# Changing the PSUM banks and the column split of one batch's hidden layer in a fused attention and MLP kernel

## The chip, the cores and the metric

The kernel runs on one core of a Trainium2 chip. The metric is device time in microseconds of one execution. The kernel before the change was timed in three runs: 244.94, 244.96 and 245.18 us, median 244.96 us. One more execution was recorded by the hardware profiler; its rows are what the text below calls the trace.

## What is computed

Eight batches of eight heads, 576 tokens and head size 64. A short sequence `p` of 32 positions per head attends to the tokens, and the tokens then attend to the 32 packed results. The output, 512 wide, goes through a two-layer network with the activation h * cos(h). Cut to its core:

```python
def sm_attn(qq, kk, vv):
    s = scale * qq @ kk.T
    a = exp(s - max(s)); a = a / sum(a)
    return a @ vv
pp  = sm_attn(p, k, v)          # 8 x 8 x 32 x 64
o   = sm_attn(q, pp, pp)        # 8 x 8 x 576 x 64
x   = o.transpose(0, 2, 1, 3).reshape(4608, 512)
h   = x @ w_in                  # 4608 x 2048
out = (h * cos(h)) @ w_out      # 4608 x 512
```

## The kernel before, in words

**Staging.** The kernel never forms `x`. For each batch b it folds the packed values into the first weight, `PPW[b] = pp @ w_in` (`ppw`, four blocks of 512 columns, n = 0 to 3), and keeps the normalised weights of the second attention, `a2n[b]` (128 rows x 2 x 576 tokens). The hidden layer of a batch is then `PPW.T @ a2n`, made in 16 pieces of 128 features, fc = 0 to 15. Each piece is two accumulated products (y = 0, 1). ScalarE (ACT) takes cos as Sin(x + pi/2) from PSUM into a `cosT` tile (three buffers), and VectorE (DVE) multiplies it with the piece in PSUM into `gT[b]`. The output layer is 16 matmuls of 512 columns per chunk of 128 tokens, four chunks per batch; the last 64 tokens of two neighbouring batches share a fifth chunk, whose input is `joint`.

**Order.** The order of the instructions on every engine is the order in which the program writes them. A batch has a "slot" (`slot`), the loop over its 16 pieces. Between the pieces, and in the stages before a slot, `fill(n)` puts n matmuls of an earlier batch's output layer, taken from the generators `out_first` (batch 0) and `out_gen` (the others). `slot` spreads the matmuls that are left by a list of weights, runs named hooks after given pieces, and at piece 10 adds the next batch's generator. So the number of output matmuls in `fill` calls ahead of slot 1 and in slot 1 add up to a constant: 33 ahead and 39 inside before the change.

**Hidden pieces.** There are two forms. `h_mm` (line 260) makes a piece over all 576 tokens, as two halves of 288 in the two banks of a pair: four matmuls of 288 columns (line 269), one cos over 576 (273) and one product over 576 (276); after pieces 7 and 15 GpSimd copies the last 64 tokens into `joint` (280). `h_one` (289) makes the first 512 tokens in a single bank: two matmuls of 512 columns (295), one cos (300), one product (301). Batch 0 uses `h_one`, and its last 64 tokens are made later, in slot 1, by `h_rest` (304): 32 matmuls of 64 columns into a pair (309), one cos and one product over 1024 columns (313, 315). Batches 1 to 7 use `h_mm`.

**PSUM.** Two of the eight banks are the output accumulators (`ot`, pool psO). The other six are handed out by `banks(kind)` (55): "pairs" gives three pairs (tags A0, A1, B), "single" six single banks (H0 to H5), "held" two pairs and two banks (psX) in which `out_first` holds chunks 2 and 3 of batch 0. Tags are used in a ring; a tile that takes a bank waits until the last reader of the tile before it is done. By the code, psX lies over H0 and H1, A0 over H2 and H3, A1 over H4 and H5, B over H0 and H1.

**Around the change** (lines 484 to 562). After batch 0's pieces: `fill(4)`, blocks 0 and 1 of `PPW[1]`, `fill(4)`, the load of the exp table, block 2, all three blocks evacuated half by ACT and half by DVE (lines 88 and 90, the helper `copy`). Then "held": 24 transposes of q of batch 1 (122), their copies to `qT`, the scores of the second attention (`s2`, 149), their sums (245), `fill`s, `normalise` (253, 255), the Sin table, and slot 1. Slot 1's hooks make block 3 of `PPW[1]`, batch 0's rest, the transposes of p (137) and of k of batch 2 (122), and issue two DMA transposes on SP's queue. When the 48th output matmul of batch 0 is in, chunk 3 is done and the pool goes from "held" to "pairs". After slot 1 come `fill(4)` and the first-attention scores of batch 2 (`s1(2)`, 149).

Of the kernel before, what the change touches and what calls it, by code (L numbers as in the profile page):

```python
# [15 lines left out]
def kernel(  # L16
# [32 lines left out]
    small = ctx.enter_context(tc.tile_pool(name="small", bufs=3))  # L49
    O = ctx.enter_context(tc.tile_pool(name="psO", bufs=2, space=PSUM))  # L50
    ctx.enter_context(tc.manual_schedule())
    psum = {"stack": ctx.enter_context(ExitStack())}

    pairs, turn = [], [0]

    def banks(kind):


        psum["stack"].close()
        for name, n in {"held": [("psX", 2), ("psA", 1)], "single": [("psH", 1)]}.get(kind, [("psB", 1), ("psA", 1)]):  # L60
            psum[name] = psum["stack"].enter_context(
                tc.tile_pool(name=name, bufs=n, space=PSUM, reuse_waits="tile"))
        pairs[:], turn[0] = (["A0", "A1"] if kind == "held" else ["A0", "A1", "B"]), 0

    banks("pairs")
    V, ACT, G = nc.vector, nc.scalar, nc.gpsimd
# [25 lines left out]
    def psa(dt=FP32):  # L92
        at = pairs[turn[0] % len(pairs)]
        turn[0] += 1
        return psum["ps" + at[0]].tile([128, 2, 512 if dt == FP32 else 1024], dt, name="psA", tag=at)
# [12 lines left out]

    def one(dt=FP32):
        turn[0] += 1  # L110
        return psum["psH"].tile([128, 512 if dt == FP32 else 1024], dt, name="psH", tag=f"H{(turn[0] - 1) % 6}")

    def pe_T(n, b, engs=(V, V, V), groups=(0, 1, 2), own=None):
        if 0 in groups:
# [186 lines left out]
            return lambda: V.tensor_tensor(out=gT[b][:, fc, 0:512], in0=ps, in1=cs, op=ALU.mult)  # L301
        return cos

    def h_rest(b):

        t = psa()
        for fc in range(NFC):
            for y in range(2):
                nc.tensor.matmul(t[:, fc // 8, (fc % 8) * 64:(fc % 8) * 64 + 64],
                                 PPW[b][:, y, fc * 128:(fc + 1) * 128], a2n[b][:, y, 512:576],  # L310
                                 start=(y == 0), stop=(y == 1))
        cs = cos_pool.tile([128, 2, 512], BF16, name="cosR", bufs=1)
        ACT.activation(out=cs, in_=t, func=AF.Sin, bias=PI_HALF)
        j0 = (b % 2) * 64
        V.tensor_tensor(out=joint[b // 2][:, :, j0:j0 + 64],
                        in0=t.rearrange("p a (f x) -> p (a f) x", x=64),
                        in1=cs.rearrange("p a (f x) -> p (a f) x", x=64), op=ALU.mult)

    osb_eng = [V]

# [44 lines left out]
    def out_first():  # L365

        pss = {}
        for c, fcs in ((0, 4), (1, 4), (2, 4), (3, 4), (0, 8), (1, 8), (2, 8), (3, 8),
                       (2, 12), (3, 12), (2, 16), (3, 16), (0, 16), (1, 16)):
            if c not in pss:  # L370
                pss[c] = (O if c < 2 else psum["psX"]).tile([128, DM], FP32, name="ot", tag="ot")
            for fc in range(8 if (c, fcs) in ((0, 16), (1, 16)) else fcs - 4, fcs):
                nc.tensor.matmul(pss[c], gT[0][:, fc, c * 128:(c + 1) * 128], w_out_bf[:, fc, :],  # L373
                                 start=(fc == 0), stop=(fc == NFC - 1))
                if fc == NFC - 1:
                    store(0, c, pss[c], V if c == 2 else ACT)
                    if c == 3:
                        banks("pairs")
                yield

    filler = []
# [101 lines left out]
    c15()()  # L483
    set_filler(0)
    fill(4)
    for n in range(2):
        ppw(1, n, (ACT, V), own=one)
    fill(4)
    ACT.preload_act_table_set(EXP_SET)
    ppw(1, 2, (ACT, V), own=one)  # L490
    banks("held")
    t = psa(BF16)
    for i in range(2):
# [10 lines left out]
    sums2(1, 0)  # L504
    fill(2)
    sums2(1, 1)
    fill(11)
    normalise(1)
    ACT.preload_act_table_set(SIN_SET)
    fill(4)  # L510
# [1 line left out]
    def slot(s, hooks, keep=0, heavy={}, last=None, trail=0, weight=None):  # L512

        left, done = to_do() - keep + trail, 0
        weight = weight or [1 + heavy.get(fc, (0, 0))[0] for fc in range(NFC)]
        for fc in range(NFC):
            rest = h_mm(s, fc)
            if fc == NFC - 1 and last:  # L520
                last()
            rest()
            if fc == 10 and trail:
                set_filler(s)
            quota = (left * sum(weight[:fc + 1])) // sum(weight) - done
            done += quota
            behind = min(quota, heavy[fc][1]) if fc in heavy else quota
            fill(quota - behind)
            while hooks and hooks[0][0] == fc:
                hooks.pop(0)[1]()  # L530
            fill(behind)
# [10 lines left out]

    def tk2():

        t = psa(BF16)
        later = []
        for i in range(2):
            later.append(pe_T("k", 2, (None,) * 3, (i,), own=lambda dt: t[:, i, :]))
        for eng, (out, ps) in zip((ACT, V), later):
            copy(eng, out, ps)  # L550

    def cross(n, b):
        return lambda: xbar(n, b)

    osb_eng[0] = ACT
    slot(1, [(5, lambda: ppw(1, 3, ACT)), (6, cross("k", 3)), (7, lambda: h_rest(0)), (9, cross("q", 2)),
             (10, lambda: pack_p(2, 4)), (12, tk2), (13, lambda: pe_T("k", 2, (V, V, ACT), (2,)))],
         trail=8, heavy={5: (0, 1), 7: (0, 4)}, weight=[3, 3, 3, 3, 3, 3, 2, 4, 2, 2, 1, 2, 1, 1, 3, 3])
    ACT.preload_act_table_set(EXP_SET)
    osb_eng[0] = V  # L560
    behind(xT["q", 2][0:1, 0, 0:1])
# [110 lines left out]
```

## Time and profile before

| | us |
|---|---|
| median of three runs | 244.96 |
| profiled execution | 244.77 |
| its span, first to last instruction | 243.0 |
| TensorE (PE) busy in the span | 233.1 |
| DVE busy | 161.9 |
| ACT busy | 167.0 |
| GpSimd (POOL) busy | 37.4 |
| slot 1 and the four output matmuls after it, by the trace | 43.38 to 64.12 |

The span lacks 1.77 us of the execution's time, which lie before the first and after the last instruction. PE is busy for 96% of the span; the granted PE clock is full in every slice. In rows of a timeline the first figure is the start and the second the length, both in us from the span's start. PEld is PE's weight load, which runs beside the matmuls. Matmuls overlap in PE's pipeline: one of 512 columns is listed with about 380 ns, but the next can start before it ends. So the cost of a matmul in a stream is the distance from one start to the next, and the rows of the chain of waits, which are cut that way, give it.

### The profile page before, as it was taken

The page shows a single profiled execution, that of the slowest core. Times are in us where ns is not written, and L with a number is a line of the kernel's source. Part 1 is how long each engine was busy: PE and PEld are TensorE (multiplying, and loading weights), DVE is VectorE, ACT ScalarE, POOL GpSimd, SP SyncE. Part 2 cuts the span into 40 slices and gives each one's busy share as a digit, 9 for nine tenths or more (in the row PEclk, how much of TensorE's full clock was granted, in tenths as well). Part 3 has the DMA queues.
Part 4 walks back from the last instruction along what each step waited for, and adds up shares of the span by engine and source line. Part 5 has one row for each costly group of instructions (what it writes and reads, how often), then busy time and mean ns, then how long its engine had stood idle before and what let it go on. Part 6 is the DMA issues. An engine that isn't in the chain of part 4 may idle for free.

```text
span 243.0 us, 5473 instructions
## 1 busy us (share of the span) xinstructions
PE 233.1 (96%) x2244; PEld 128.2 (53%) x2244; DVE 161.9 (67%) x256; ACT 167.0 (69%) x266; POOL 37.4 (15%) x60
## 2 busy tenths in 40 slices
PE   7789889999999999999999999999999999999994
PEld 3454335566545564566546564556456554565453
DVE  3359993568568886687857786677758787887001
ACT  2349899588749868876878677877788683776110
POOL 8522212210130005005100501030100110010000
PEclk9999999999999999999999999999999999999999
DMA  6999999999899999998999896989284102311133
GB/s 94 202 205 206 205 206 227 193 215 189 189 162 163 240 197 139 219 213 159 234 205 199 163 212 117 193 161 214 60 175 112 46 0 46 86 43 46 46 84 86
DMA packets 64376, 37.37 MB, mean 154 GB/s; under 512 B 36864, under 2 KB 59776, under 8 KB 64352
## 3 DMA queue, kind: packets, MB, share of 16 engines
q0 software_dynamic: 23152, 18.75, 51.5%
q1 hardware_dynamic: 40960, 18.16, 35.7%
q8 instruction: 17, 0.28, 0.5%
q10 hardware_dynamic: 240, 0.13, 0.2%
q14 instruction: 7, 0.06, 0.1%
HBM read 37.22 MB, written 9.44 MB: 192 GB/s over the span
## 4 chain that ended last, share of the span: by engine, by line
PE 83%; DVE 8%; ACT 3%; DMA 3%; issue 1%; ACTq 0%; POOLq 0%
PE ot L360 45%; PE psA L269 21%; PE ot L373 4%; DVE gT L301 3%; DMA kbf<-in_k_dram 3%; PE psA L219 3%; PE psA L149 2%; PE psA L245 2%; DVE gT L276 2%; DVE PPW L90 2%; PE ot L343 1%; PE psA L192 1%; PE psA L122 1%; ACT cosT L273 1%; DVE a2n L255 1%
## 5 line engine op out<-in xcount | busy, mean ns | idle before, releaser
L360 PE MATMUL ot<-w_out_bf,gT 128*128 128x512 bf16 x448 | 114.9, 379 | 0.0
L276 DVE TENSOR_TENSOR gT<-psA,cosT 128x576 bf16<-128x576 f32 x112 | 83.5, 757 | 22.2 <-ACT cosT L273 21.1
L273 ACT ACTIVATE cosT<-psA 128x576 bf16<-128x576 f32 x112 | 72.9, 652 | 25.1 <-PE psA L269 23.6
L269 PE MATMUL psA<-a2n,PPW 128*128 128x288 bf16 x448 | 73.2, 286 | 0.2 <-DVE gT L276 0.2
L360 PEld LDWEIGHTS <-gT 128*128 128x128 bf16 x448 | 42.2, 98 | 37.8 <-issue 4.2
L269 PEld LDWEIGHTS <-PPW 128*128 128x128 bf16 x448 | 43.8, 98 | 29.9 <-issue 1.0
L90 DVE CAST PPW<-psA 128x1024 bf16<-128x1024 f32 x19 | 23.0, 1221 | 7.9 <-PE psA L219 7.9
L90 DVE COPY osb<-ot 128x512 f32<-128x512 f32 (+2 forms) x18 | 11.7, 648 | 16.0 <-PE ot L343 14.6
L280 POOL COPY joint<-gT 128x512 bf16<-128x512 bf16 x14 | 8.6, 615 | 87.4 <-DVE gT L276 87.4
L88 ACT COPY osb<-ot 128x512 f32<-128x512 f32 (+1 forms) x20 | 11.3, 567 | 14.5 <-PE ot L360 12.2
L255 DVE SCALAR_TENSOR_TENSOR a2n<-a2u,r,lns 128x576 bf16<-128x576 bf16 x16 | 12.4, 815 | 12.3 <-ACT lns L253 12.3
L373 PE MATMUL ot<-w_out_bf,gT 128*128 128x512 bf16 x64 | 17.0, 380 | 0.3 <-DMA w_out_bf<-in_moe_w_out_dram 0.3
L158 ACT ACTIVATE a<-psA 128x576 bf16<-128x576 f32 x16 | 10.3, 647 | 7.7 <-PE psA L149 7.7
L247 ACT ACTIVATE lns<-psA 128x576 f32<-128x576 f32 x16 | 10.4, 651 | 7.4 <-PE psA L245 6.8
L360 PE MATMUL ot<-w_out_bf,joint 128*128 128x512 bf16 x48 | 14.6, 379 | 0.0
L237 ACT ACTIVATE a2u<-psA,rs 128x576 bf16<-128x576 f32 x16 | 11.0, 737 | 1.4 <-PE psA L149 1.4
L103 POOL COPY gate<-kT 1x1 bf16<-1x1 bf16 x4 | 0.7, 178 | 66.2 <-DMA kT<-kbf 66.2
L301 DVE TENSOR_TENSOR gT<-psH,cosT 128x512 bf16<-128x512 f32 x16 | 9.9, 685 | 0.4 <-ACT cosT L300 0.4
L253 ACT ACTIVATE lns<-lns 128x576 f32<-128x576 f32 x16 | 10.0, 673 | 0.0
L412 PE MATMUL ot<-wz 128*128 128x512 f32 (+2 forms) x13 | 7.7, 683 | 1.9 <-DVE wz L425 1.7
L300 ACT ACTIVATE cosT<-psH 128x512 bf16<-128x512 f32 x16 | 8.9, 631 | 0.7 <-DVE gT L301 0.7
L295 PE MATMUL psH<-a2n,PPW 128*128 128x512 bf16 x32 | 8.2, 381 | 1.0 <-DVE PPW L90 1.0
(89 smaller groups left out, 186.4 us busy)
## 6 DMA issues: line engine op xcount, KB each, us to landing
kbf<-in_k_dram POOLq DMA_DIRECT2D x8, 576.0 KB, 13.1
vbf<-in_v_dram POOLq DMA_DIRECT2D x8, 576.0 KB, 7.5
qbf<-in_q_dram POOLq DMA_DIRECT2D x8, 576.0 KB, 10.4
out_dram<-osb SPq DMA_DIRECT2D x24, 192.0 KB, 2.5
out_dram<-osb SPq DMA_DIRECT2D x22, 128.0 KB, 2.7
w_in_bf<-in_moe_w_in_dram POOLq DMA_DIRECT2D x4, 512.0 KB, 17.0
w_out_bf<-in_moe_w_out_dram POOLq DMA_DIRECT2D x4, 512.0 KB, 21.3
out_dram<-osb SPq DMA_DIRECT2D x25, 64.0 KB, 2.3
```

Of the source, the lines that this page charges most:

```text
L88: ACT.copy(out=out, in_=in_)
L90: eng.tensor_copy(out=out, in_=in_)
L158: ACT.activation(out=a1[b % 2][:, y, :, 0:TP].rearrange("p (e m) x -> p e m x", e=2), in_=ps[y][:, :, 0:HS].rearrange("p e (m x) -> p e m ...
L237: ACT.activation(out=a2u[b][:, y].rearrange("p (e x) -> p e x", e=2), in_=ps[y][:, :, 0:HS], func=AF.Exp, scale=rs1[b][:, y:y + 1])
L247: ACT.activation(out=lns[b][:, y].rearrange("p (e x) -> p e x", e=2), in_=ps[:, :, 0:HS], func=AF.Ln)
L255: V.scalar_tensor_tensor(out=a2n[b][:, y], in0=a2u[b][:, y], scalar=r1[b][:, y:y + 1], in1=lns[b][:, y], op0=ALU.mult, op1=ALU.mult)
L269: nc.tensor.matmul(ps[:, e, 0:HS], PPW[b][:, y, fc * 128:(fc + 1) * 128], a2n[b][:, y, e * HS:(e + 1) * HS], start=(y == 0), stop=(y == 1))
L273: ACT.activation(out=csv, in_=ps[:, :, 0:HS], func=AF.Sin, bias=PI_HALF)
L276: V.tensor_tensor(out=gT[b][:, fc, :].rearrange("p (e x) -> p e x", e=2), in0=ps[:, :, 0:HS], in1=csv, op=ALU.mult)
L301: return lambda: V.tensor_tensor(out=gT[b][:, fc, 0:512], in0=ps, in1=cs, op=ALU.mult)
L360: nc.tensor.matmul(ps, w, w_out_bf[:, fc, :], start=(fc == 0), stop=(fc == NFC - 1))
L373: nc.tensor.matmul(pss[c], gT[0][:, fc, c * 128:(c + 1) * 128], w_out_bf[:, fc, :], start=(fc == 0), stop=(fc == NFC - 1))
```

## The change

Batch 1's pieces are made by `h_one` instead of `h_mm`, in single banks. `h_rest` becomes `h_half(b, a)`: 16 matmuls of 64 columns for eight pieces into one single bank, one cos and one product over 512 columns. Slot 1 calls it four times, for both halves of batch 0 and of batch 1; the two copies into `joint` on GpSimd go. Slot 1 begins in a new layout "four" (single banks over H2 to H5, while psX still holds the two chunks) and goes to six single banks when the 48th output matmul is in, with the ring set to go on at H3. The single banks are reserved in order when the layout starts. Block 3 of `PPW[1]` moves from piece 5 to piece 7, into two single banks, evacuated by ACT and DVE instead of ACT alone; the transposes of p and k take single banks, and the third copy of k goes from ACT to DVE. Ahead of the slot, blocks 0, 1 and 2 of `PPW[1]` take H2 and H3, H0 and H1, H4 and H5 (before: H0 and H1, H2 and H3, H4 and H5), and two output matmuls move from `fill(11)` into the slot: 31 ahead, 41 inside. After the slot the layout is "pairs", its ring at A0.

```diff
@@ -49,18 +49,24 @@
     small = ctx.enter_context(tc.tile_pool(name="small", bufs=3))
     O = ctx.enter_context(tc.tile_pool(name="psO", bufs=2, space=PSUM))
     ctx.enter_context(tc.manual_schedule())
-    psum = {"stack": ctx.enter_context(ExitStack())}
-
-    pairs, turn = [], [0]
+    psum, inner, outer = {}, ctx.enter_context(ExitStack()), ExitStack()
+
+    pairs, turn, ring = [], [0], [6]
 
     def banks(kind):
 
 
-        psum["stack"].close()
-        for name, n in {"held": [("psX", 2), ("psA", 1)], "single": [("psH", 1)]}.get(kind, [("psB", 1), ("psA", 1)]):
-            psum[name] = psum["stack"].enter_context(
-                tc.tile_pool(name=name, bufs=n, space=PSUM, reuse_waits="tile"))
+        inner.close()
+        if kind != "four":
+            outer.close()
+        for name, n, st in {"held": [("psX", 2, outer), ("psA", 1, inner)], "four": [("psH", 1, inner)],
+                            "single": [("psH", 1, inner)]}.get(kind, [("psB", 1, inner), ("psA", 1, inner)]):
+            psum[name] = st.enter_context(tc.tile_pool(name=name, bufs=n, space=PSUM, reuse_waits="tile"))
         pairs[:], turn[0] = (["A0", "A1"] if kind == "held" else ["A0", "A1", "B"]), 0
+        ring[0] = 4 if kind == "four" else 6
+        if kind in ("four", "single"):
+            for i in range(ring[0]):
+                psum["psH"].tile([128, 512], FP32, name="psH", tag=f"H{i}")
 
     banks("pairs")
     V, ACT, G = nc.vector, nc.scalar, nc.gpsimd
@@ -108,7 +114,7 @@
 
     def one(dt=FP32):
         turn[0] += 1
-        return psum["psH"].tile([128, 512 if dt == FP32 else 1024], dt, name="psH", tag=f"H{(turn[0] - 1) % 6}")
+        return psum["psH"].tile([128, 512 if dt == FP32 else 1024], dt, name="psH", tag=f"H{(turn[0] - 1) % ring[0]}")
 
     def pe_T(n, b, engs=(V, V, V), groups=(0, 1, 2), own=None):
         if 0 in groups:
@@ -301,20 +307,19 @@
             return lambda: V.tensor_tensor(out=gT[b][:, fc, 0:512], in0=ps, in1=cs, op=ALU.mult)
         return cos
 
-    def h_rest(b):
-
-        t = psa()
-        for fc in range(NFC):
+    def h_half(b, a):
+
+        t = one()
+        for f in range(8):
+            fc = 8 * a + f
             for y in range(2):
-                nc.tensor.matmul(t[:, fc // 8, (fc % 8) * 64:(fc % 8) * 64 + 64],
-                                 PPW[b][:, y, fc * 128:(fc + 1) * 128], a2n[b][:, y, 512:576],
-                                 start=(y == 0), stop=(y == 1))
-        cs = cos_pool.tile([128, 2, 512], BF16, name="cosR", bufs=1)
+                nc.tensor.matmul(t[:, f * 64:f * 64 + 64], PPW[b][:, y, fc * 128:(fc + 1) * 128],
+                                 a2n[b][:, y, 512:576], start=(y == 0), stop=(y == 1))
+        cs = cos_pool.tile([128, 512], BF16, name="cosT")
         ACT.activation(out=cs, in_=t, func=AF.Sin, bias=PI_HALF)
         j0 = (b % 2) * 64
-        V.tensor_tensor(out=joint[b // 2][:, :, j0:j0 + 64],
-                        in0=t.rearrange("p a (f x) -> p (a f) x", x=64),
-                        in1=cs.rearrange("p a (f x) -> p (a f) x", x=64), op=ALU.mult)
+        V.tensor_tensor(out=joint[b // 2][:, 8 * a:8 * a + 8, j0:j0 + 64], in0=t.rearrange("p (f x) -> p f x", x=64),
+                        in1=cs.rearrange("p (f x) -> p f x", x=64), op=ALU.mult)
 
     osb_eng = [V]
 
@@ -375,7 +380,8 @@
                 if fc == NFC - 1:
                     store(0, c, pss[c], V if c == 2 else ACT)
                     if c == 3:
-                        banks("pairs")
+                        banks("single")
+                        turn[0] = 3
                 yield
 
     filler = []
@@ -483,11 +489,12 @@
     c15()()
     set_filler(0)
     fill(4)
-    for n in range(2):
+    for n, at in ((0, 2), (1, 0), (2, 4)):
+        turn[0] = at
+        if n == 2:
+            fill(4)
+            ACT.preload_act_table_set(EXP_SET)
         ppw(1, n, (ACT, V), own=one)
-    fill(4)
-    ACT.preload_act_table_set(EXP_SET)
-    ppw(1, 2, (ACT, V), own=one)
     banks("held")
     t = psa(BF16)
     for i in range(2):
@@ -504,7 +511,7 @@
     sums2(1, 0)
     fill(2)
     sums2(1, 1)
-    fill(11)
+    fill(9)
     normalise(1)
     ACT.preload_act_table_set(SIN_SET)
     fill(4)
@@ -516,7 +523,7 @@
         left, done = to_do() - keep + trail, 0
         weight = weight or [1 + heavy.get(fc, (0, 0))[0] for fc in range(NFC)]
         for fc in range(NFC):
-            rest = h_mm(s, fc)
+            rest = h_one(s, fc)() if s == 1 else h_mm(s, fc)
             if fc == NFC - 1 and last:
                 last()
             rest()
@@ -542,10 +549,9 @@
 
     def tk2():
 
-        t = psa(BF16)
         later = []
         for i in range(2):
-            later.append(pe_T("k", 2, (None,) * 3, (i,), own=lambda dt: t[:, i, :]))
+            later.append(pe_T("k", 2, (None,) * 3, (i,), own=one))
         for eng, (out, ps) in zip((ACT, V), later):
             copy(eng, out, ps)
 
@@ -553,9 +559,14 @@
         return lambda: xbar(n, b)
 
     osb_eng[0] = ACT
-    slot(1, [(5, lambda: ppw(1, 3, ACT)), (6, cross("k", 3)), (7, lambda: h_rest(0)), (9, cross("q", 2)),
-             (10, lambda: pack_p(2, 4)), (12, tk2), (13, lambda: pe_T("k", 2, (V, V, ACT), (2,)))],
-         trail=8, heavy={5: (0, 1), 7: (0, 4)}, weight=[3, 3, 3, 3, 3, 3, 2, 4, 2, 2, 1, 2, 1, 1, 3, 3])
+    banks("four")
+    slot(1, [(5, lambda: h_half(0, 0)), (6, cross("k", 3)), (6, lambda: h_half(0, 1)),
+             (7, lambda: ppw(1, 3, (ACT, V), own=one)), (9, cross("q", 2)), (9, lambda: h_half(1, 0)),
+             (10, lambda: pack_p(2, 4, one(BF16))), (11, lambda: h_half(1, 1)), (12, tk2),
+             (13, lambda: pe_T("k", 2, (None, None, V), (2,), own=one))],
+         trail=8, heavy={5: (0, 1), 6: (0, 1), 7: (0, 1), 9: (0, 1), 11: (0, 1)},
+         weight=[3, 3, 3, 4, 4, 2, 2, 2, 3, 2, 2, 2, 1, 2, 3, 3])
+    banks("pairs")
     ACT.preload_act_table_set(EXP_SET)
     osb_eng[0] = V
     behind(xT["q", 2][0:1, 0, 0:1])
```

## The prediction

> **What bounds the kernel now.** I read the page first, to see which engine fills the span.
>
> ```profile
> span 243.0 us, 5473 instructions
> ...
> PE 233.1 (96%) x2244; PEld 128.2 (53%) x2244; DVE 161.9 (67%) x256; ACT 167.0 (69%) x266; POOL 37.4 (15%) x60
> ...
> PE 83%; DVE 8%; ACT 3%; DMA 3%; issue 1%; ACTq 0%; POOLq 0%
> ```
>
> PE is busy nearly always, and the chain of waits that sets the end runs 83% through it. So time can be won by less PE work or where PE stands still, and nowhere else. Next the table of stretches, for slot 1 with the four output matmuls after it.
>
> ```profile
> 43.38:64.12 20.74, 20.23 (x176) 12.64 (x175) 14.58 (x20) 15.73 (x25) 2.21 (x3) 1.00 1.31 208
> ```
>
> Its columns are length, then busy time of PE, PEld, DVE, ACT and POOL. Busy PE hides short stops, because a matmul is listed longer than its share of the stream. What a matmul costs stands in the chain in order of time:
>
> ```profile
> 40.30 3.24 PE ot L373 x15
> ...
> 43.54 0.49 PE psA L269 x4
> ...
> 52.38 0.93 PE psA L309 x32
> ```
>
> A 512-column matmul takes 3.24/15 = 0.216 us of the stream, a piece in four matmuls of 288 takes 0.49, a 64-column one 0.93/32 = 0.029. With these I walked PE's timeline through slot 1 and looked for starts that come later than the one before plus its cost:
>
> ```profile
> 49.44 0.75 DVE L276 TENSOR_TENSOR gT<-psA,cosT 128x576 bf16<-128x576 f32 x1
> ...
> 49.56 0.59 PE L373 MATMUL ot<-w_out_bf,gT 128*128 128x512 bf16 x2
> ...
> 50.24 0.41 PE L219 MATMUL psA<-w_in_bf,ppT 64*32 64x512 bf16 x8
> ...
> 56.57 0.38 PE L373 MATMUL ot<-w_out_bf,gT 128*128 128x512 bf16 x1
> ...
> 57.12 0.65 PE L269 MATMUL psA<-a2n,PPW 128*128 128x288 bf16 x4 [0.17 <-DVE gT L276]
> ...
> 59.43 0.65 PE L269 MATMUL psA<-a2n,PPW 128*128 128x288 bf16 x4
> 59.52 0.76 DVE L276 TENSOR_TENSOR gT<-psA,cosT 128x576 bf16<-128x576 f32 x1 [0.27 <-ACT cosT L273]
> ...
> 60.33 0.50 PE L122 MATMUL psA<-ident,kbf 96*128 96x96 bf16 x8 [0.25 <-DVE gT L276]
> ...
> 62.52 1.67 PE L360 MATMUL ot<-w_out_bf,gT 128*128 128x512 bf16 x7
> ...
> 64.12 0.44 PE L149 MATMUL psA<-kT,P 64*32 64x288 bf16 x16
> ```
>
> There are three stops. Block 3 of PPW starts at 50.24 instead of 49.56 + 0.43 = 49.99: 0.25 late, just behind the product that ends at 50.19 and frees its pair. Of this 0.09 is the step from full to 64-row matmuls, which stays: at 64.12 it costs 64.12 - 62.52 - 7 x 0.216 = 0.09 with no bank in the way. That leaves **0.16**. Piece 11 starts at 57.12 instead of 56.79: **0.33**. The third group of k starts at 60.33 instead of 59.43 + 0.49 = 59.92: **0.41**, behind the product that ends at 60.28. All three wait for a pair of banks until the product in it is done. Together 0.90 us.
>
> **The change part by part.** *PE's work*: before, 16 x 0.49 + 0.93 = 8.77 us for batch 1's pieces and batch 0's rest. After, 32 x 0.216 + 64 x 0.029 = 8.77. The columns are the same, so nothing is won or lost here. The two output matmuls moved into the slot are neutral as well (33 + 39 = 31 + 41).
>
> *Ahead of the slot.* Here the pair that the q transposes take is freed one block sooner:
>
> ```profile
> 15.37 0.79 POOL L99 DMA_DIRECT2D qbf<-in_q_dram  x1 [3.45 <-PE psA L122]
> ```
> ```profile
> DMA to landing us min/median/max: 20.1/20.1/20.1
> ```
> ```profile
> 34.50 1.88 DVE L90 CAST PPW<-psH 128x512 bf16<-128x512 f32 x3
> ...
> 35.10 0.41 PE L219 MATMUL psH<-w_in_bf,ppT 64*32 64x512 bf16 x8
> ...
> 35.90 1.06 PEld L122 LDWEIGHTS <-qbf 96*128 96x128 bf16 x24 [0.69 <-DMA qbf<-in_q_dram]
> 35.93 0.84 PE L122 MATMUL psA<-ident,qbf 96*128 96x96 bf16 x16 [0.42 <-DVE PPW L90]
> 36.43 0.59 ACT L88 CAST PPW<-psH 128x512 bf16<-128x512 f32 x1
> 36.60 0.50 PE L122 MATMUL ot<-ident,qbf 96*128 96x96 bf16 x8
> ...
> 37.15 0.80 ACT L88 COPY qT<-ot 128x768 bf16<-128x768 bf16 x1
> ...
> 37.90 0.51 PE L149 MATMUL psA<-qT,ppT 64*32 64x288 bf16 x16
> ```
>
> DVE's three casts start 0.60 apart and end at 35.18, 35.78 and 36.38. The transposes wait for the second; after the change for the first, and then for q itself, whose load lands at 15.37 + 20.1 = 35.5. So they start at 35.5 instead of 35.93, 0.4 sooner. But the scores need the third copy of qT too, which is ACT's: it waits for the cast at 36.43, which sits behind a table load, and can start at 37.02, or at 36.92 if ACT's operations overlap as DVE's 0.68 at 0.60 apart do, instead of at 37.15. So the bounds are 0.13 by ACT and 0.40 by the transposes, and I take **0.2**, ACT's better case. The chain to `a2n` moves by as much:
>
> ```profile
> 41.60 1.55 DVE L255 SCALAR_TENSOR_TENSOR a2n<-a2u,r,lns 128x576 bf16<-128x576 bf16 x2 [3.83 <-ACT lns L253]
> ```
>
> With two output matmuls fewer, PE, which was there at 43.38, reaches the second matmul of piece 0 at 43.38 - 0.2 - 0.43 + 0.22 = 42.97, and `a2n` ends at 43.15 - 0.2 = 42.95. That costs some 0.03 us.
>
> *Evacuation.* The prices, by group and shape:
>
> ```profile
> L276 DVE TENSOR_TENSOR gT<-psA,cosT 128x576 bf16<-128x576 f32 x112 | 83.5, 757 | 22.2 <-ACT cosT L273 21.1
> L273 ACT ACTIVATE cosT<-psA 128x576 bf16<-128x576 f32 x112 | 72.9, 652 | 25.1 <-PE psA L269 23.6
> ...
> L301 DVE TENSOR_TENSOR gT<-psH,cosT 128x512 bf16<-128x512 f32 x16 | 9.9, 685 | 0.4 <-ACT cosT L300 0.4
> ...
> L300 ACT ACTIVATE cosT<-psH 128x512 bf16<-128x512 f32 x16 | 8.9, 631 | 0.7 <-DVE gT L301 0.7
> ...
> L315 DVE TENSOR_TENSOR joint<-psA,cosR 128x1024 bf16<-128x1024 f32 x1 | 1.2, 1225 | 0.6 <-ACT cosR L313 0.6
> L309 PEld LDWEIGHTS <-PPW 128*128 128x128 bf16 x32 | 1.1, 98 | 0.0
> ```
>
> DVE: before 16 x 0.757 + 1.225 = 13.3; after 20 x 0.685 = 13.7. The product of a half (512 columns into pieces of 64 of `joint`) isn't in the trace. It is bounded by half of L315, 0.61, and by the longer L276, 0.757; I take L301's 0.685, the same size. DVE also gets half of block 3 (0.68, a cast of those above) and the third copy of k (0.56, its row is with the rivals). In sum DVE gains 1.6 us, 14.6 to 16.2, in a stretch that PE fills for 19.8 (20.74 - 0.9). ACT: 20 x 0.631 = 12.6 against 16 x 0.652 and one of double width, at most 1.26, in sum 11.7; the copy of k (0.80, as that of qT above) and half of the block leave it. So it stays about where it is, 15.7. Both stay under PE, so I cost this at nothing; the cover is PE's own stream, and what it costs without that is the third rival. On POOL two copies go that nobody waited for.
>
> *The three waits.* By the code, the singles in order are: pieces 0 to 4 on H2, H3, H4, H5, H2; then piece 5 on H3, half H4, piece 6 H5, half H0, piece 7 H1, block 3 H2 and H3, pieces 8 and 9 H4 and H5, half H0, piece 10 H1, p H2, piece 11 H3, half H4, piece 12 H5, k on H0 and H1, piece 13 H2, third k H3, pieces 14 and 15 H4 and H5. A bank comes back after four tiles, later six, where it was a pair after two or three. Block 3 takes banks of pieces 4 and 5, two pieces and two halves old. Piece 11 takes the bank of block 3. The third k is the closest: it takes piece 11's bank. Between them PE issues a half (16 x 0.029), piece 12 (0.43), two groups of k (0.67, as the 16 transposes of q from 35.93 to 36.60), piece 13 (0.43) and three output matmuls (0.65): 2.6 us. Piece 11 is evacuated 0.16 + 0.63 + 0.69, with waits 1.6 us, after its last start. So all three stops go, and DVE may lag by about 1 us before one comes back.
>
> *What is late next.* `s1(2)` takes A0, then A1, and A1 now holds piece 15. From piece 15's last start PE has 0.22, seven output matmuls (1.51), the step (0.09) and the first half of the scores (0.18): 2.0 us. Its cos and product are done 0.38 + 0.63 + 0.69, with hand-overs 1.8 us, after it. That is 0.2 us to spare; I cost it at nothing.
>
> *The sum*: 0.16 + 0.33 + 0.41 + 0.2 - 0.03 = 1.07, 1.1 us. After slot 1 the chain is PE's, so the gain should last to the end. The profiled execution took 244.77, its span and 1.77 around it: 243.7. The median stands 0.19 above it, so the forecast is 244.96 - 1.1 = **243.9**.
>
> **The rivals.** *Partly* (0.12): one of the longer stops comes back, because a product is late in its new place, or ACT holds the front. For it speaks the 1 us of slack above, which halves and copies share. The gain is 0.5 to 0.7: 244.3.
>
> *Given back later* (0.08): PE comes 1.1 us sooner to work that DMAs pace. The tightest that I found is a1T of batch 3:
>
> ```profile
> 71.21 5.11 SPq L172 DMA_TRANSPOSE a1T<-a  x1
> ```
> ```profile
> DMA to landing us min/median/max: 11.1/11.1/11.1
> ```
> ```profile
> 84.02 0.56 PE L192 MATMUL psA<-vbf,a1T 96*32 96x64 bf16 x48
> ```
>
> It lands at 82.3 and is needed at 84.02, then at 82.9: 0.6 left, if the transfer doesn't move at all. A landing that slips by 0.6 and more takes the gain back, to 244.6 to 245.0.
>
> *DVE becomes the bound* (0.06): in the slot it has 20 products and some other work:
>
> ```profile
> L90 DVE COPY osb<-ot 128x512 f32<-128x512 f32 x16 | 11.0, 685 | 1.4 <-DMA out_dram<-osb 1.4
> ...
> L90 DVE COPY kT<-psA 128x768 bf16<-128x768 bf16 x3 | 1.7, 558 | 2.3 <-PE psA L122 2.2
> ...
> L139 DVE COPY P<-psA 128x512 bf16<-128x512 bf16 x2 | 0.8, 420 | 2.5 <-PE psA L137 2.5
> ```
>
> Half of block 3 (0.60), chunk 2, two copies of k and p make 2.8 us. At 0.60 apart that is 14.8 of 19.6, so up to 0.24 more per product is hidden. Beyond 0.24 each 0.1 costs 2 us, and at 0.30 more the change is slower than before. If the halves, stepping through `joint`, and the single-bank products came 0.95 apart, between L301 and L315, DVE would need 21.8: 2.2 us late, 246.1. Against it: batch 0's products of this very size came 0.60 apart, as the casts do.
>
> *Short matmuls wait for their weights* (0.04): each of the 64 needs its own load of 98 ns, for 0.029 of matmul. In the 32 of L309 the loads ran beside each other. If in groups of 16 they did not, the added 32 would cost 32 x (0.098 - 0.029) = 2.2 us more: 246.1. It decides from 0.034 per matmul on. The Trainium skill speaks for a part of it: "TensorE: Matmul & The Clock Gate", section "Back-to-back issue gap", gives about 81 ns for each pair of weight load and 128-column matmul in a sustained stream. By that the added 32 would take 1.7 us more, and the kernel 245.5, slower. The trace disagrees, with 29 ns for each of 32 in a row, and I go by it.
>
> **How the numbers follow.** The forecast has 0.70 (243.6 to 244.1, from the front's bounds and the spread of the runs), the rivals 0.12, 0.08, 0.06 and 0.04. A measurement can tell about 0.2%, 0.5 us, so the line is at 244.47. Faster: the forecast and the partial gain, 0.82, less 0.02 for a part that falls short: 0.80. The same: 0.10, the gain given back and that part. Slower: 0.10, the last two. The range 243.5 to 244.5 holds the first two cases.
>
> **What would show it.** The rows of PE in slot 1 should show no wait for a product ahead of block 3, piece 11 and the third group of k, and `s1(2)` should start at about 63.0 instead of 64.12. The q transposes should start at 35.5 and the scores after them at 37.7 or sooner. Busy DVE should rise by about 1.6 us in the slot. Wrong would be: a wait for a1T ahead of 83, a wait at `s1(2)`, 64-column matmuls over 0.03 apart, or products over 0.8 apart.

## The result, and the profile after

The changed kernel takes 243.71 us in the median of five runs (243.59 to 244.22), the kernel before 244.96 in five runs beside it (244.85 to 245.18): a ratio of 0.9953, with a 95% interval of 0.9939 to 0.9968. The gain is 1.25 us, where 1.1 was forecast. The profiled execution of the changed kernel was the longest of the five, 244.22 us with a span of 242.4, against 244.77 and 243.0 before. (Of one experiment below, four of twelve executions had a granted TensorE clock of 0.95 or 0.993, which is part of why its times lie far apart.)

The page of the changed kernel: span, busy time by engine, and the shares of the chain that ended last.

```profile
span 242.4 us, 5480 instructions
...
PE 232.9 (96%) x2244; PEld 126.0 (52%) x2244; DVE 162.8 (67%) x261; ACT 166.5 (69%) x268; POOL 36.2 (15%) x58
...
PE 83%; DMA 8%; DVE 4%; ACT 2%; issue 1%; POOLq 0%
```

PE has the same number of matmuls and the same busy time, and DVE's share of the chain went from 8% to 4%. DMA's went from 3% to 8%, which is one step of the chain, told further down. The table of stretches for slot 1 with the four matmuls after it, in the changed kernel (length, then PE, PEld, DVE, ACT and POOL busy):

```profile
42.75:63.06 20.31, 20.31 (x179) 10.55 (x177) 16.13 (x26) 15.84 (x27) 1.59 (x2) 1.00 1.29 203
```

It is 0.43 us shorter than the 20.74 before, and holds two output matmuls more (2 x 0.216 = 0.43). So at equal work it won 0.86 us. It also begins at 42.75 instead of 43.38, which is 0.63 sooner; 0.43 of that are the same two matmuls, which no longer stand ahead of it, and 0.20 is won there (0.07 of it by a first output matmul that starts sooner, at 32.53 instead of 32.60, where the trace before waited 0.32 for the load of `w_out`). Together 1.06 us at the start of `s1(2)`, 63.06 against 64.12. The chain of waits in order of time shows the slot without a stop (a row of the chain begins where the one before it ends, so its times lie up to 0.2 us behind the starts in a timeline):

```profile
49.42 0.47 PE psH L316 x16
...
51.87 0.21 PE ot L378
52.08 0.34 PE psH L225 x8
...
56.24 0.43 PE psH L301 x2
...
58.90 0.43 PE psH L301 x2
59.33 0.34 PE psH L128 x8
...
61.62 1.51 PE ot L365 x7
63.13 0.37 PE psA L155 x16
```

From 43.4 to 63 us this chain has only PE rows, each beginning where the one before ends and as long as its matmuls' cost (behind block 3 with the step, 0.1). Block 3 (L225), piece 11 (56.24) and the third group of k (L128 at 59.33), which stood still before, follow at once. The timeline of the changed kernel ahead of the slot, and at its end:

```profile
35.50 1.06 PEld L128 LDWEIGHTS <-qbf 96*128 96x128 bf16 x24 [0.25 <-DMA qbf<-in_q_dram]
35.53 0.84 PE L128 MATMUL psA<-ident,qbf 96*128 96x96 bf16 x16
...
36.94 0.80 ACT L94 COPY qT<-ot 128x768 bf16<-128x768 bf16 x1
...
37.50 0.72 PE L155 MATMUL psA<-qT,ppT 64*32 64x288 bf16 x16
...
37.80 0.12 PEld L155 LDWEIGHTS <-ppT 64*32 64x32 bf16 x9 [0.19 <-issue]
```
```profile
62.28 0.69 DVE L307 TENSOR_TENSOR gT<-psH,cosT 128x512 bf16<-128x512 f32 x1 [0.18 <-ACT cosT L306]
...
63.06 0.44 PE L155 MATMUL psA<-kT,P 64*32 64x288 bf16 x16
```

The transposes of q start 0.40 sooner and now wait for q's load instead of DVE. The scores (L155) start at 37.50 instead of 37.90, but halt after some matmuls: their list of weights breaks off and goes on at 37.80, just behind ACT's copy, which ends at 36.94 + 0.80 = 37.74. At the slot's end, piece 15's product ends at 62.97, and the second half of `s1(2)`, 0.18 after 63.06, is what needs its bank.

What is won at 63.06 isn't all there at the end: the span is 0.6 shorter, not 1.06. The chain shows where the rest is:

```profile
70.14 13.30 DMA a1T<-a
83.48 0.56 PE psA L198 x48
```

The transposed a1 of batch 3 was issued at 70.14, 1.07 sooner than before, and landed at 83.44, 1.1 later than before (82.3). PE waited for it, as the timeline's row says:

```profile
83.48 0.56 PE L198 MATMUL psA<-vbf,a1T 96*32 96x64 bf16 x48 [0.46 <-DMA a1T<-a]
```

From `s1(2)` to the end of the trace this execution took 179.36 us, where the one before took 178.84: 0.52 given back, by this wait. Two more executions of the changed kernel, below, took 178.84 as well.

### The profile page after: what moved, and what is told of

It is laid out like the page before. It is cut to its first block, busy times and chain, and to the rows that moved or that the text cites. A ratio compares the mean times of both kernels' runs of the same rounds, so it can differ in the third digit from the quotient of the medians.

```text
span 242.4 us, 5480 instructions
## 1 busy us (share of the span) xinstructions
PE 232.9 (96%) x2244; PEld 126.0 (52%) x2244; DVE 162.8 (67%) x261; ACT 166.5 (69%) x268; POOL 36.2 (15%) x58
## 4 chain that ended last, share of the span: by engine, by line
PE 83%; DMA 8%; DVE 4%; ACT 2%; issue 1%; POOLq 0%
PE ot L365 42%; PE psA L275 17%; PE ot L378 6%; DMA a1T<-a 5%; PE psH L301 4%; DMA kbf<-in_k_dram 3%; PE psA L155 2%; PE psA L225 2%; PE psA L251 2%; PE psA L198 1%; PE ot L348 1%; DVE gT L307 1%; DVE PPW L96 1%; PE psA L128 1%; PE psH L316 1%; DVE a2n L261 1%
## 5 line engine op out<-in xcount | busy, mean ns | idle before, releaser
L282 DVE TENSOR_TENSOR gT<-psA,cosT 128x576 bf16<-128x576 f32 x96 | 71.4, 757 | 16.3 <-ACT cosT L279 15.3
L279 ACT ACTIVATE cosT<-psA 128x576 bf16<-128x576 f32 x96 | 62.4, 652 | 21.3 <-PE psA L275 20.0
L275 PE MATMUL psA<-a2n,PPW 128*128 128x288 bf16 x384 | 62.7, 286 | 0.0
L275 PEld LDWEIGHTS <-PPW 128*128 128x128 bf16 x384 | 37.5, 98 | 25.4 <-issue 0.6
L307 DVE TENSOR_TENSOR gT<-psH,cosT 128x512 bf16<-128x512 f32 x32 | 21.0, 688 | 4.5 <-ACT cosT L306 4.4
L306 ACT ACTIVATE cosT<-psH 128x512 bf16<-128x512 f32 x32 | 18.5, 615 | 4.6 <-PE psH L301 3.5
L301 PE MATMUL psH<-a2n,PPW 128*128 128x512 bf16 x64 | 17.7, 380 | 1.0 <-DVE PPW L96 1.0
L286 POOL COPY joint<-gT 128x512 bf16<-128x512 bf16 x12 | 7.3, 616 | 64.6 <-DVE gT L282 64.6
L253 ACT ACTIVATE lns<-psA 128x576 f32<-128x576 f32 x16 | 10.4, 651 | 7.4 <-PE psA L251 6.8
L301 PEld LDWEIGHTS <-PPW 128*128 128x128 bf16 x64 | 5.8, 98 | 8.3 <-DVE PPW L96 2.0
```

The lines of the kernel that those rows point to most:

```text
L275: nc.tensor.matmul(ps[:, e, 0:HS], PPW[b][:, y, fc * 128:(fc + 1) * 128], a2n[b][:, y, e * HS:(e + 1) * HS], start=(y == 0), stop=(y == 1))
L279: ACT.activation(out=csv, in_=ps[:, :, 0:HS], func=AF.Sin, bias=PI_HALF)
L282: V.tensor_tensor(out=gT[b][:, fc, :].rearrange("p (e x) -> p e x", e=2), in0=ps[:, :, 0:HS], in1=csv, op=ALU.mult)
L301: nc.tensor.matmul(ps, PPW[b][:, y, fc * 128:(fc + 1) * 128], a2n[b][:, y, 0:512], start=(y == 0), stop=(y == 1))
L306: ACT.activation(out=cs, in_=ps, func=AF.Sin, bias=PI_HALF)
```

## The experiments

The theory is that of the prediction: the stops go because a bank is older when a tile takes it, and the front gives a little. Rivals are that the order of the banks ahead of the slot does it, that DVE is near its limit, and, for the wait at a1T, that a load issued ahead of the transposes holds them up. Kernels that are compared with the same time of the kernel before shared its runs and the chip.

**The front alone.** In the kernel before, the packed blocks ahead of slot 1 take the new banks; the slot stays.

```diff
-    for n in range(2):
+    for n, at in ((0, 2), (1, 0), (2, 4)):
+        turn[0] = at
+        if n == 2:
+            fill(4)
+            ACT.preload_act_table_set(EXP_SET)
         ppw(1, n, (ACT, V), own=one)
-    fill(4)
-    ACT.preload_act_table_set(EXP_SET)
-    ppw(1, 2, (ACT, V), own=one)
```

> The kernel before with the order of banks of blocks 0 to 2 of PPW[1] changed, and nothing else (33 output matmuls ahead of slot 1, 39 inside). If the wait of the q transposes for DVE's cast is what goes, and ACT's copy of qT then holds the scores: transposes at 35.5 instead of 35.93, scores done and piece 0 reached 0.2 us sooner, 0.2 us off the time (244.75). If ACT does not hold it, 0.4 off (244.55). If the front is hidden anyway (piece 0 waits for a2n in any case): no change. The three stops in slot 1 stay as they are, 0.16, 0.33 and 0.41.

Measured: 244.91 against 244.91, ratio 0.9995 (0.9986 to 1.0003), the runs in two groups, 244.48 to 244.64 and 244.91 to 245.18. By this alone the front gains nothing that can be told. It was run again beside its counterpart:

> The front alone once more, since its first times fell into two groups (244.5 to 244.6 and 244.9 to 245.2) around a median of no change, while its trace had the scores of batch 2 0.23 us sooner after the first output matmul (31.29 against 31.52). If the 0.23 is real and the upper group is chance of the loads: a median near 244.7. If something takes it back in most executions: 244.9 again.

Measured: 244.62 against 244.86, ratio 1.0005 (0.9988 to 1.0022; one run of 246.82 widens it). The medians differ by 0.24, but neither interval leaves out no change. The trace of this second run shows the effect, though, and that the slot's stops stay when the front alone is changed (timeline, PE):

```profile
35.50 0.85 PE L122 MATMUL psA<-ident,qbf 96*128 96x96 bf16 x16
...
49.33 0.59 PE L373 MATMUL ot<-w_out_bf,gT 128*128 128x512 bf16 x2
...
50.01 0.41 PE L219 MATMUL psA<-w_in_bf,ppT 64*32 64x512 bf16 x8
...
56.90 0.65 PE L269 MATMUL psA<-a2n,PPW 128*128 128x288 bf16 x4 [0.17 <-DVE gT L276]
...
60.11 0.50 PE L122 MATMUL psA<-ident,kbf 96*128 96x96 bf16 x8 [0.25 <-DVE gT L276]
...
63.90 0.44 PE L149 MATMUL psA<-kT,P 64*32 64x288 bf16 x16
```

Block 3 comes 0.25 after its turn (49.33 + 0.43), and piece 11 and k wait for products by the same 0.17 and 0.25 idle as before. `s1(2)` starts 0.22 sooner than in the kernel before.

**The slot alone.** The changed kernel with the blocks in the old banks:

```diff
-    for n, at in ((0, 2), (1, 0), (2, 4)):
+    for n, at in ((0, 0), (1, 2), (2, 4)):
```

> The changed kernel with blocks 0 to 2 of PPW[1] on the banks they had before. If the two parts add up: transposes at 35.93 again, no stop in slot 1, 0.9 us off the time (244.05), 0.2 short of the whole change. If the front is worth 0.4: 0.7 off. If the slot gains by something else than its waits, the sum with the front alone will not be the whole.

Measured: 244.07 against 244.91, ratio 0.9973 (0.996 to 0.9987). Its profiled execution, at 246.06, reached the first output matmul only at 34.31, over 1 us later than any other, and isn't read. Again:

> The slot alone once more, for a trace that is not disturbed ahead of the slot (in the first one the q transposes stood 1.2 us instead of 0.8). From the first output matmul to the scores of batch 2: 31.52 less 0.86, 30.66; time 244.07 again, and 243.7 for the whole change.

Measured: 244.05 against 244.86, ratio 0.9968 (0.9955 to 0.998). That is 0.81 us from the slot. Its stretch has the length of the changed kernel's to the hundredth (table of stretches), and the front is the old one (timeline):

```profile
43.11:63.42 20.31, 20.31 (x180) 10.57 (x178) 16.13 (x26) 15.84 (x27) 1.59 (x2) 1.00 1.30 196
```
```profile
36.09 0.84 PE L128 MATMUL psA<-ident,qbf 96*128 96x96 bf16 x16 [0.70 <-DVE PPW L96]
...
63.42 0.44 PE L155 MATMUL psA<-kT,P 64*32 64x288 bf16 x16
```

So the stops are the slot's, and the slot's part alone takes them away. Against this run the new front is worth 63.42 - 63.06 = 0.36 us; against the trace of before it was 0.2. From the first output matmul to `s1(2)` this run took 30.93 where 30.66 was expected. The missing 0.27 is in the front: the casts of the blocks started 2.17 behind the first output matmul (34.66 - 32.49), in the trace of before 1.90 (34.50 - 32.60). That shifts the old front and not the new one, whose transposes wait for q's load.

**Four banks instead of six.** The changed kernel, where the layout goes on with H2 to H5 after batch 0 is done. It tells whether the age of the banks is what removed the stops.

```diff
-                        turn[0] = 3
+                        turn[0], ring[0], base[0] = 1, 4, 2
```

> The changed kernel, but the slot goes on with the four banks H2 to H5 after the 48th output matmul, instead of six. If the number of tiles in the ring decides: the third group of k waits for piece 11's product again, about 0.2 us, and piece 8 some 0.06; 0.3 us slower than the changed kernel, still 0.8 faster than before. If it is the single bank with its shorter product alone (a pair was held by a whole piece), no stop comes back and the time is the changed kernel's.

Measured: 244.0 against 244.91, ratio 0.9967 (0.9954 to 0.998). The third group of k is late again (timeline):

```profile
58.68 0.69 DVE L307 TENSOR_TENSOR gT<-psH,cosT 128x512 bf16<-128x512 f32 x1
...
58.78 0.59 PE L301 MATMUL psH<-a2n,PPW 128*128 128x512 bf16 x2
...
59.43 0.50 PE L128 MATMUL psH<-ident,kbf 96*128 96x96 bf16 x8
```

59.43 - 58.78 is 0.65 where two matmuls cost 0.43: a stop of 0.22, where the changed kernel has 59.17 - 58.74 = 0.43 and none. With one of 0.06 at piece 8 and one of 0.03 at piece 13 the stops are 0.30 us in this trace (its stretch, 42.73 to 63.31, is 0.27 longer than the changed kernel's), and the ring of four still beats the pairs.

The bank that the third group of k takes here is by the code H5, that of piece 12, and not piece 11's as expected. Piece 12's product ends at 58.68 + 0.69 = 59.37, and k starts 0.06 later. In the kernel before, too, k took the bank of piece 12 and piece 11 that of piece 9. So with four banks the two take the banks of the same pieces as before, and yet piece 11's stop of 0.33 is gone and k's 0.41 is 0.22. Of piece 11 the traces show why. A half (0.47) and an output matmul now stand between the pieces 9 and 10, and from piece 9's start to piece 11's turn pass 2.42 us instead of 1.85, while piece 9's product ends 1.96 behind its start (before 2.13, with the product of 1.23 us for batch 0's rest ahead of it). For k it is 1.79 us to its turn (before 1.87), and the product ends after 1.95 (before 2.23). In the changed kernel k takes piece 11's bank, free at 58.03 and taken at 59.17. So the change without its two extra banks removes most of the stops, and these two the rest. The other parts of the slot's change (block 3 later and evacuated by two engines, a copy of k moved from ACT to DVE) weren't tested by themselves.

**DVE's slack.** A copy of 128, then of 256 columns behind each of the 20 products in slot 1; nobody reads what it writes.

```diff
+                if b == 1:
+                    V.tensor_copy(out=scr[:, 0:128], in_=wz4[:, 0:128])
...
+        V.tensor_copy(out=scr[:, 0:128], in_=wz4[:, 0:128])
```

> The changed kernel with one more DVE operation (a copy of 128 x 128 from fp32 to bf16 into a tile that nobody reads) behind each of the 20 products of slot 1: about 0.13 us of DVE each, 2.6 us in all. If PE's stream covers DVE as the prediction has it (0.24 per product to spare): no stop in slot 1, and the time of the changed kernel within 0.1. If DVE already bounds the slot: 1 to 2.6 us slower.

> The same with 128 x 256: about 0.23 us of DVE each, 4.6 us in all. If the slack is 0.24 per product over the whole slot: at its edge; DVE ends the slot late, the scores of batch 2 wait for piece 15's product, and the time is up by 0 to 1.2 us. If DVE had far more room: no change. If it is bound already: 4 us or more.

Measured: with 128 columns 244.24 against 244.93, ratio 0.9973 (0.9961 to 0.9985); with 256 columns 244.64, ratio 0.999 (0.9981 to 0.9998); the changed kernel beside them 244.19. The timeline, with 128 columns and then with 256:

```profile
51.34 0.68 DVE L309 TENSOR_TENSOR gT<-psH,cosT 128x512 bf16<-128x512 f32 x1
51.94 0.21 DVE L311 CAST scr<-wz 128x128 bf16<-128x128 f32 x1
52.08 0.68 DVE L326 TENSOR_TENSOR joint<-psH,cosT 128x512 bf16<-128x512 f32 x1
```
```profile
51.42 0.68 DVE L309 TENSOR_TENSOR gT<-psH,cosT 128x512 bf16<-128x512 f32 x1
52.02 0.28 DVE L311 CAST scr<-wz 128x256 bf16<-128x256 f32 x1
52.22 0.68 DVE L326 TENSOR_TENSOR joint<-psH,cosT 128x512 bf16<-128x512 f32 x1
...
61.54 0.60 ACT L306 ACTIVATE cosT<-psH 128x512 bf16<-128x512 f32 x1 [0.48 <-PE psH L301]
...
62.88 0.68 DVE L309 TENSOR_TENSOR gT<-psH,cosT 128x512 bf16<-128x512 f32 x1
...
63.61 0.32 PE L155 MATMUL psA<-kT,P 64*32 64x288 bf16 x8 [0.35 <-DVE gT L309]
```

A product still takes 0.60 of DVE's stream (51.34 to 51.94), and the copy adds 0.14 or 0.20, so products follow each other at 0.74 and 0.80 where nothing else holds them. At 0.74 the trace has no stop in the slot and `s1(2)` at 63.00. At 0.80 piece 15's product starts at 62.88 instead of 62.28, and the second half of `s1(2)` waits for it. From `s1(2)` to the end that execution took 179.40 instead of 178.84, 0.56 more. So in these traces the slack per product lies between 0.14 and 0.20, and what is late first is the last product, not one inside the slot. Its cosine was done at 62.14, so what it waited for is DVE's own queue of work.

**The transfer that gave back.** Batch 4's k is loaded later, behind a1 of batch 3, so that it is issued after the DMA transposes.

```diff
-    load("k", 4)
...
+    behind(a1[1][0:1, 1, 0, 0:1])
+    load("k", 4)
```

> The changed kernel, with the load of k of batch 4 issued after the DMA transpose of a1 of batch 3 instead of ahead of it. In the profiled execution of the changed kernel PE waited 0.5 us for that transpose, which landed 0.4 us after the load of k. If the transpose stands behind the load in the DMA engines: it lands at 80 or sooner, PE waits for it in no run, and all runs lie near 243.6. If the DMA was only slow in that execution, or the transpose is slow by itself: it lands as late as before, and the runs spread as the changed kernel's, 243.6 to 244.2.

Measured: 245.85 against 244.91 (243.71 to 250.6), ratio 1.0005 (0.9981 to 1.0029). The times lie too far apart to tell anything; in its trace the transposes landed 9.4 us after issue. Again, beside the changed kernel unaltered:

> The load of k of batch 4 behind the DMA transpose of a1 of batch 3, once more: of its first runs most had TensorE slowed. If the transpose stands behind that load: it lands 2 to 3 us ahead of PE's need in any execution, no wait at the packed values of batch 3, 243.6 in undisturbed runs. If that load does not hold it: as the changed kernel beside it.

> The changed kernel once more, unaltered, beside the experiments of this job. If PE's wait for the DMA transpose of a1 of batch 3 comes from how fast the loads run in an execution: in this profile it is gone or another length, and the runs spread from 243.6 (no wait) to 244.2. If it belongs to the kernel: 0.5 us again.

Measured: the later load 245.39 (244.79 to 248.08) against 244.93, ratio 1.0038 (1.001 to 1.0066), slower; the changed kernel 244.19, ratio 0.9961 (0.9948 to 0.9973). The theory was that the load of k ahead of the transposes held them up. The chain of the later load speaks against it:

```profile
70.50 13.50 DMA a1T<-a
84.05 0.55 PE psA L198 x48
```

The transposes were issued at 70.50, the load of k only at 71.17, and they landed at 84.0, the latest of all. So the order of issue doesn't decide it: the same kernel had 9.4 us in the one execution and 13.5 in the other. Whether the load slows them by running beside them isn't tested. The wait of about 0.7 and a first output matmul that came late, at 32.99, explain the span of 243.0 in this trace. But this execution took 244.8, one of the two shortest, and why the median is 1.2 us longer than the changed kernel's stays open. The changed kernel unaltered had no wait for a1T in this run (issued at 70.65, landed at 80.8), but its profiled execution took 244.22 as well. All its work was late from the first output matmul on, with the slot no longer than 20.31, because that matmul waited for the load of `w_out` (timeline):

```profile
33.15 1.04 PE L378 MATMUL ot<-w_out_bf,gT 128*128 128x512 bf16 x4 [0.74 <-DMA w_out_bf<-in_moe_w_out_dram]
```

**Work ahead of the wait.** In slot 2 of the changed kernel, the packing of batch 3, which waits for a1T, moves from piece 7 to piece 9, two pieces later.

```diff
-    slot(2, [(7, lambda: tiled(2))], 0, {7: (6, 4)}, lambda: pp_T(3, V))
+    slot(2, [(7, blocks2), (8, lambda: held8.append(spare[0])), (9, lambda: pp(3, V, own=lambda: held8[0]))],
+         0, {7: (6, 4), 9: (0, 0)}, lambda: pp_T(3, V))
```

> The changed kernel, with the packed values of batch 3 made after piece 9 of slot 2 instead of after piece 7 (in the spare columns of piece 8's pair). They need the DMA transpose of a1 of batch 3, and come 2 us later. If the spread of the changed kernel above 243.7 comes in part from PE's wait for that transpose: no such wait in any profile, fewer times at 244.2, and 0.1 us lost for one more step between full and narrow matmuls: 243.7 to 243.8. If the spread comes from the landing of w_out and q ahead of slot 1 alone: the times stay spread from 243.7 to 244.3.

> The changed kernel beside it, unaltered: 243.6 to 244.2 again. From the first output matmul of batch 0 to the scores of batch 2, 30.4 to 30.5 us (before: 31.5) in any execution; what differs between executions lies ahead of the one or after the other.

Measured: 244.43 against 244.99, ratio 0.9978 (0.9968 to 0.9989); the changed kernel beside it 243.73 (243.65 to 243.77, six runs), ratio 0.9944 (0.9928 to 0.996). The move costs 0.7 us. Its timeline shows where most of it goes:

```profile
85.36 0.76 DVE L282 TENSOR_TENSOR gT<-psA,cosT 128x576 bf16<-128x576 f32 x1 [1.01 <-ACT cosT L279]
85.39 0.38 PE L365 MATMUL ot<-w_out_bf,joint 128*128 128x512 bf16 x1
86.17 0.55 PE L198 MATMUL psA<-vbf,a1T 96*32 96x64 bf16 x48 [0.40 <-DVE gT L282]
```

After piece 9 the packing takes the pair of piece 8, whose product ends at 86.12, and PE waits for that: it starts 0.78 behind a matmul that costs 0.22, 0.56 late with the step. So a wait for a bank came in, and no run of the twelve was under 244.28. The changed kernel itself, beside it, had no wait for the transposes and no time above 243.77, so this job can't say whether the move would have helped in an execution that has the wait. Its transposes and the row that needs them:

```profile
L178 SPq DMA_TRANSPOSE a1T<-a x1: 4122/4122/4122, 70.1 to 70.1; - x1
...
DMA to landing us min/median/max: 10.4/10.4/10.4
```
```profile
82.90 0.56 PE L198 MATMUL psA<-vbf,a1T 96*32 96x64 bf16 x48
```

They landed at 80.5, 2.4 before they were needed. No version beat the changed kernel.

## Why the prediction was right, point by point

| us from the span's start | before | after | after, second | after, third | slot alone |
|---|---|---|---|---|---|
| first output matmul | 32.60 | 32.53 | 33.15 | 32.50 | 32.49 |
| transposes of q | 35.93 | 35.53 | 36.05 | 35.47 | 36.09 |
| piece 0 | 43.38 | 42.75 | 43.26 | 42.69 | 43.11 |
| `s1(2)` | 64.12 | 63.06 | 63.57 | 63.00 | 63.42 |
| first output matmul to `s1(2)` | 31.52 | 30.53 | 30.42 | 30.50 | 30.93 |
| a1T of batch 3 landed | 82.3 | 83.4 | 80.8 | 80.5 | 80.7 |
| `s1(2)` to the end | 178.84 | 179.36 | 178.84 | 178.84 | 178.84 |

*The three stops* (0.16 + 0.33 + 0.41, less 0.03 for `a2n`): right in size, and right that they are waits for banks. The sum 0.87 stands against 20.74 + 0.43 - 20.31 = 0.86 in the traces, and 0.81 and 0.84 in the times of the slot alone. The front alone leaves the stops where they were, and the slot alone takes them away. That the deeper ring does it is shown for k, of which 0.22 comes back with four banks. It is not the whole account: piece 11's stop and half of k's go even with four banks, where they take the banks of the same pieces as before, because more matmuls stand between the two uses of the bank (piece 11) or the product ends sooner (k). For block 3 the parts (later place, two single banks) weren't separated.

*The front* (0.2, bounds 0.13 and 0.40): counted from the first output matmul to piece 0, less the two matmuls that moved, the three traces of the changed kernel won 0.13, 0.24 and 0.16 against the trace of before, and 0.40 to 0.51 against the slot alone. ACT holds it as forecast, with the copy that ends at 37.74. In the times it can't be told from nothing by itself, and the sum of the two parts' medians, 0.24 + 0.81 = 1.05 (in the first pair 0.00 + 0.84), stays 0.2 to 0.4 below the 1.25 of the whole; with intervals of this width that stays open. That the sum of the forecast, 1.07, met the 1.06 of the trace to 0.01 is partly luck: from the first output matmul to `s1(2)` the three executions of the changed kernel won 0.99, 1.10 and 1.02.

*PE's work is equal*: 16 matmuls of 64 columns took 0.47, 0.029 each, in groups of 16 as in one of 32, so the short ones didn't wait for their weights. That was the place of the Trainium skill's rule ("TensorE: Matmul & The Clock Gate", section "Back-to-back issue gap", about 81 ns for a pair of weight load and matmul of 128 columns). The trace goes against it here too: matmuls of half that width came 0.029 apart, each with a weight load of its own, and the four transposes of p, such pairs of 128 columns, took 0.22 in the chain, 0.055 each. The prices of evacuation, in the list of groups of the changed kernel (shapes apart):

```profile
L321 DVE TENSOR_TENSOR joint<-psH,cosT 128x512 bf16<-128x512 f32 x4 | 2.8, 692 | 0.0
L316 PE MATMUL psH<-a2n,PPW 128*128 128x64 bf16 x64 | 2.5, 193 | 0.0
L316 PEld LDWEIGHTS <-PPW 128*128 128x128 bf16 x64 | 2.4, 98 | 0.9
```

The product into `joint` took 692 ns, where 685 was taken and 0.61 to 0.757 bounded it. DVE's busy time in the slot rose by 1.55 us (14.58 to 16.13; 1.6 forecast), and ACT's stayed (15.73 to 15.84).

*DVE hides*: right, but with less room than written. The working spread DVE's slack evenly, 0.24 per product; the runs showed a stop already at 0.20. (The 19.6 us that it set DVE's work against isn't derived and leaves out the two matmuls that moved into the slot; with the measured 20.31 the mean would be 0.27.) The slack isn't even. In the changed kernel DVE stands idle 0.39 ahead of each of several early products, waiting for their cosines, and can't use that time later. In the trace with 256 columns it works without a pause from 57.95 on, with both copies of k among the products, and so reaches the last one late. *`s1(2)` has 0.2 to spare*: the last product ends at 62.97 and is needed at 63.24, 0.27.

*Given back later* (0.08, with 244.6 to 245.0): the mechanism is real, and it struck one of the three profiled executions of the changed kernel, with 0.52 us of the 1.06. The prediction took 0.6 of slack "if the transfer doesn't move at all"; it moved, by 1.1 us the wrong way though issued 1.07 sooner. Of 16 runs of the changed kernel, 11 took 243.58 to 243.77 and five 243.98 to 244.22. The two profiled ones among the five had different causes, one this wait, one the late load of `w_out`. So the price was put too high, as the longest time was 244.22; one execution in three is too few to judge the chance. Why the same transposes take 9.4 to 13.5 us stays open: the order of issue with the load of k doesn't decide it, and moving the work that waits cost 0.7 us.

## What to carry to other kernels

When an engine is busy 96% of a span, look for the few starts that come later than the one before plus its cost; three such stops here gave 0.86 us by the traces without any less work. Smaller tiles in a deeper ring cost PE nothing here, as the columns stayed the same. For each stop, compare two times: that from the last use of the bank to the turn of the tile that takes it, and that from the same use to the end of its product. The engine's mean load says neither. Before moving work away from a wait that only some executions show, see which bank it will take in its new place: here a wait of 0.5 us, seen in one of three, was answered by a move that cost 0.7 us in the median.

## What was not expected of the hardware

The same DMA transposes, issued between 70.1 and 71.4 us, took 9.4 to 11.1 us to land in ten of the twelve traces that show it, and 13.3 and 13.5 in the other two. The view of the DMAs from 70 to 84 us shows the difference between the first profiled execution of the changed kernel, with 13.3, and then the third, with 10.4. The rows are packets, MB and share of the 16 engines' time, for the software queue, which brings the loads, and the hardware queue, which makes the transposes and carries the outputs:

```profile
q0 software_dynamic: 1993, 1.49, 79.2%
q1 hardware_dynamic: 2402, 0.85, 48.6%
```
```profile
q0 software_dynamic: 1900, 1.42, 66.8%
q1 hardware_dynamic: 5145, 1.52, 58.0%
```

A MB of loads took 53% of the engines' time in the one and 47% in the other, a MB of the hardware queue 57% and 38%. The later load, with 13.5 us, has 53% and 68%; the second trace of the changed kernel, with 10.1, has 47% and 39%. So a MB took longer on both queues in the two slow cases, most on the hardware queue, whose mix of transposes and outputs may differ. What slowed them, the traces don't show.
